# A range check of the softmax sums, with a branch to a short f32 path, at the end of a gated recurrence with soft mixture of experts

## The chip, the cores and the metric

The kernel runs on one core of one Trainium2 chip. The time is device microseconds of that core, the median of three runs. The profile is of one execution, and its times count from the start of its span.

## The reference, cut to what matters

Four sequences of 5056 tokens with 256 channels go through a gated linear recurrence. Its output feeds a soft mixture of 8 experts with 4 slots each, so 32 slots. Every slot takes a softmax over all 20224 tokens, every token one over the 32 slots.

```python
f = lower_bound + (1 - lower_bound) * sigmoid(f_logit);  i = 1 - f
for t in range(S):                       # S = 5056, B = 4, D = 256
    h = f[:, t] * h + i[:, t] * x[:, t];  y[:, t] = h
x = y.reshape(B * S, D)
logits = x @ phi                         # phi: 256 x 32, drawn at 0.05
d = exp(logits - logits.max(0));  d /= d.sum(0) + 1e-9
slot_in = (d.T @ x).reshape(8, 4, D)
slot_out[e] = maximum(slot_in[e] @ w1[e], 0) @ w2[e]      # 1024 hidden
c = exp(logits - logits.max(1));  c /= c.sum(1) + 1e-9
out = c @ slot_out                       # 20224 x 256, f32
```

The input x is drawn at 0.1 times a standard normal, f_logit around 2, lower_bound between 0.4 and 0.7.

## The kernel before, in words

The tokens go through in groups of 512 for each sequence. VectorE runs the recurrence as scans along time, with channels on partitions (L345), and TensorE turns tiles between tokens and channels (L263, L277, L358). The kernel takes its exponentials **without subtracting a maximum**: `etall` holds exp(logits) in bf16 for all tokens, with a sequence's 32 slots on 32 partitions. Two kinds of sums are kept of them. Each row sum, over the 32 slots of a token, is inverted and held in `rrow`, a tile of 128 x 40 x 4 f32. The column sums, over the tokens, are collected by group in `csum` and added up in `cs1` (L670). The order of all instructions is written out by hand (`manual_schedule`), and each engine works through its own queue.

From about 122 us the experts' weights arrive, and the slots' outputs are computed. The last weights are in at 140.48; then TensorE ends `so_ps` (L749), VectorE makes `slot_pre` and `slot_so` (L746, L747) and `slot_out` (L784), and GpSimd `slot_bd`. From there on the output is made. A piece of it is one small product of 32 or 64 slots with the exponentials (L813, L850), scaled by `rrow` on the way from PSUM to an output tile in turns by ScalarE and VectorE (L855, L858), and stored by SyncE's DMA queue. The helper `whole` makes the output of one sequence, `couple` that of two, for 2048 tokens; `couple` writes a tile `oc` of 128 x 2 x 16 x 256 f32 and issues two stores of 2048 KB, one for each sequence (L870). The last three calls of `couple` come last in the program, so its last two stores are those of the last call, first sequence then second. The tiles come from the pool `osb` with three buffers, the PSUM tiles from `pout` with eight.

Behind the last store the program leaves through line 927 (the exit of the tile context). There SyncE waits for all outstanding transfers and for the other engines, ten wait instructions in the built program, then drains, and two barriers over the five engines follow. Between the barriers GpSimd clears the semaphores.

```python
cs1 = ew.tile([P, 1], F32, name="cs1")                    # L669
nc.vector.tensor_reduce(cs1, csum, AX.X, ALU.add)
...
for i in range(end):                                      # end = 2
    for j in range(B // 2):
        if i or j < B // 2 - 1:
            couple(i, j)
```

Of the kernel before, what the change touches and what calls it, by code (L numbers as in the profile page):

```python
# [14 lines left out]
PSUM = bass.MemoryType.PSUM  # L15


@with_exitstack
def kernel(
# [58 lines left out]
    lbs = consts.tile([P, 4, DC], F32, name="lbs")  # L78
    omlb, nomlb = lbs[:, 0], lbs[:, 1]
# [43 lines left out]
    rrow = store.tile([P, n_grp * R, B], F32, name="rrow")  # L123
# [50 lines left out]
    with tc.tile_pool(name="sp2", bufs=3) as sp2, \  # L174
# [21 lines left out]
        xs, fs, sts, uts, pss, psus, hs, hps, hts, lgs, ets = ({} for _ in range(11))  # L196
# [438 lines left out]
        hid, wide = cleared["hid"], cleared["wide"]  # L635
        hid = hid.rearrange("p (f e s) -> p f e s", f=FC, s=NS)
# [17 lines left out]
        for o in range(DC):  # L654
            nc.tensor.matmul(sin_ps[:, o], slot_v[:, o], rep[:, 0],
                             start=True, stop=True, skip_group_check=True)

    with tc.tile_pool(name="ew", bufs=1) as ew, \
# [5 lines left out]
        sin = [ew.tile([P, NS], BF16, name=f"sin{o}") for o in range(DC)]  # L664
# [1 line left out]
        nc.scalar.activation(sin[1], sin_ps[:, 1], ACT.Copy, scale=omlb[:, ds(1, 1)])  # L666
        row_sums(8, 14)

        cs1 = ew.tile([P, 1], F32, name="cs1")  # L669
        nc.vector.tensor_reduce(cs1, csum, AX.X, ALU.add)  # L670


# [22 lines left out]
        for q in range(E // Q):  # L695
# [47 lines left out]
        for j in range(Q):  # L743
            for fc in range(FC):
                if j == Q - 1 and fc == half:
# [5 lines left out]
                                 start=(j, fc) in ((0, 0), (Q - 1, half)),  # L751
# [45 lines left out]


    held.close()
    with tc.tile_pool(name="osb", bufs=3, reuse_waits="tile") as osb:  # L800

        def by_vector(ob, op, scale):
            nc.vector.tensor_tensor(ob, op, scale.broadcast_to(list(ob.shape)), ALU.mult)

        def by_scalar(ob, op, scale):
            for i in range(ob.shape[1]):
                nc.scalar.activation(ob[:, i], op[:, i], ACT.Copy, scale=scale[:, i])  # L807

        def share(op, i, b, r, k):
            t0, n_r = blocks[i]  # L810
            ew = etall[ds(b * NS, NS), ds(t0, P * n_r)].rearrange("s (p r) -> s p r", r=n_r)
            for j in range(k):
                nc.tensor.matmul(op[:, j], ew[:, :, r + j], slot_out[ds(b * NS, NS)],  # L813
                                 start=True, stop=True, skip_group_check=True)

        def scale_of(i, b, r, k):
            return rrow[:, ds(blocks[i][0] // P + r, k), ds(b, 1)]

        def rows_of(i, b):
            t0, n_r = blocks[i]  # L820
            return out[ds(b * S + t0, P * n_r)].rearrange("(p r) d -> p r d", r=n_r)

        pout = ctx.enter_context(tc.tile_pool(name="pout", bufs=8, space=PSUM, reuse_waits="tile"))

        def whole(i, b, pieces, ends):
            n_r = blocks[i][1]
            dst = rows_of(i, b)
            ob = osb.tile([P, n_r, D], F32, name="ob", tag="ob")
            done = pieces[0][1]
            for j, r, k in pieces:  # L830
                op = pout.tile([P, 2, D], F32, name="op", tag="op")
                share(op, i, b, r, k)
                (by_vector, by_scalar)[j](ob[:, ds(r, k)], op[:, ds(0, k)],
                                          scale_of(i, b, r, k))
                if r + k in ends:
                    q = ds(done, r + k - done)
                    nc.sync.dma_start(out=dst[:, q], in_=ob[:, q])
                    done = r + k

        def couple(i, j, ends=()):  # L840
            t0, n_r = blocks[i]
            ends = ends or (n_r,)
            ew = etall[ds(j * 2 * NS, 2 * NS), ds(t0, P * n_r)].rearrange(
                "s (p r) -> s p r", r=n_r)
            scale = rrow[:, ds(t0 // P, n_r), ds(2 * j, 2)]
            ob = osb.tile([P, 2, n_r, D], F32, name="oc", tag="oc")
            done = 0
            for r in range(n_r):
                op = pout.tile([P, 2, D], F32, name="op", tag="op")
                nc.tensor.matmul(op.rearrange("p u d -> p (u d)"), ew[:, :, r],  # L850
                                 slot_bd[ds(j * 2 * NS, 2 * NS)].rearrange("s u d -> s (u d)"),
                                 start=True, stop=True, skip_group_check=True)
                if r % 7 in (1, 4, 6):
                    for u in range(2):
                        nc.scalar.activation(ob[:, u, r], op[:, u], ACT.Copy,  # L855
                                             scale=scale[:, r, ds(u, 1)])
                else:
                    nc.vector.tensor_tensor(  # L858
                        ob[:, :, r], op,
                        scale[:, r].unsqueeze(2).broadcast_to([P, 2, D]), ALU.mult)  # L860
                if r + 1 in ends:
                    q = ds(done, r + 1 - done)
                    if done:
                        both = out[ds(2 * j * S, 2 * S)].rearrange(
                            "(u t) d -> u t d", u=2)[:, ds(t0, P * n_r)].rearrange(
                            "u (p r) d -> p u r d", r=n_r)
                        nc.sync.dma_start(out=both[:, :, q], in_=ob[:, :, q])
                    else:
                        for u in range(2):
                            nc.sync.dma_start(out=rows_of(i, 2 * j + u)[:, q],  # L870
                                              in_=ob[:, u, q])
                    done = r + 1

        def rest():
            n_p = B // 2
            ob = osb.tile([P, n_p, D], F32, name="ob", tag="ob")
            dst = out.rearrange("(b t) d -> t b d", b=B)
            for j in range(n_p):
                k = ds(j * 2 * NS, 2 * NS)
                op = pout.tile([P, 2, D], F32, name="op", tag="op")  # L880
# [51 lines left out]
```

## Time and profile before

| | |
|---|---|
| median of 3 runs | 196.48 us (196.40 to 197.11) |
| the profiled execution's own time | 196.48 us |
| its span | 194.7 us (194.69), 1.79 less |
| busy: TensorE, VectorE, ScalarE, GpSimd | 149.7, 145.7, 140.9, 104.9 us |
| read from and written to HBM | 58.23 and 20.71 MB, 405 GB/s over the span |
| last compute instruction starts | 174.56 us |
| last store issued | 175.11 us |

The page of the profile cuts the span in 40 slices of 4.87 us and gives the busy share of each engine in tenths. "SPq" is SyncE's instruction queue, "DVE" is VectorE, "ACT" ScalarE, "PE" TensorE's matmuls and "PEld" its weight loads, "POOL" GpSimd. A row of waits names who waited, for whom, the sum in us, how often, and the longest. In the answer for one line, the three numbers behind a count are the shortest, median and longest duration in ns, followed by the start of the first and of the last.

### The profile page before, as it was taken

To read this page: it belongs to the slowest core of one execution; us is meant where nothing else is said; L and a number is where in the kernel's file an instruction comes from. 1 tells how busy PE (TensorE), PEld (TensorE's weight loads), DVE (VectorE), ACT (ScalarE), POOL (GpSimd) and SP (SyncE) were. 2 spreads that over 40 slices of the span, in tenths; PEclk is the share of its full clock that TensorE was granted. 3 is DMA by queue.
4 is the path that set the end of the run, shared out by engine and by line. 5 is a ranking of instruction groups with operands and counts; after the bars stand their busy time and mean duration, and the time that the engine had idled before them with its cause. 6 is when DMAs were issued, how large, how long until landed. Compare 5 with 4: busy or idle time off the path is not lost.

```text
span 194.7 us, 3288 instructions
## 1 busy us (share of the span) xinstructions
PE 149.7 (77%) x1203; PEld 103.9 (53%) x1204; DVE 145.7 (75%) x197; ACT 140.9 (72%) x204; POOL 104.9 (54%) x82
## 2 busy tenths in 40 slices
PE   2777797988999889789789868999898999970000
PEld 1655666765786767657576746567775333210000
DVE  2259899999799999999999999525199799760000
ACT  3199678899998999999988797644269987770000
POOL 2369679774999778884978988484030000000000
PEclk9999999999999999999999999999999555555555
DMA  5999999999999999999999999999949999999995
GB/s 204 415 418 423 427 429 421 428 431 380 351 429 422 411 328 422 431 425 353 382 415 407 264 223 214 213 215 213 181 175 422 429 432 431 431 431 431 431 431 219
DMA packets 13281, 70.75 MB, mean 363 GB/s; under 512 B 1473, under 2 KB 2242, under 8 KB 9298
## 3 DMA queue, kind: packets, MB, share of 16 engines
q1 hardware_dynamic: 10352, 62.13, 76.7%
q0 software_dynamic: 2912, 8.42, 21.9%
q8 instruction: 9, 0.15, 0.3%
q14 instruction: 6, 0.05, 0.1%
q10 hardware_dynamic: 2, 0.00, 0.0%
HBM read 58.23 MB, written 20.71 MB: 405 GB/s over the span
## 4 chain that ended last, share of the span: by engine, by line
DVE 24%; DMA 22%; PE 18%; ACT 11%; issue 8%; POOL 7%; ACTq 0%; POOLq 0%; DVEq 0%
DVE h L345 16%; DMA w_t<-in_moe_w_dram 9%; PE op L850 9%; POOL u_t L253 6%; DMA x_t<-in_x_dram 5%; DMA w_sb<-in_moe_w_dram 5%; ACT oc L855 5%; DVE ht L377 4%; DVE h L337 3%; DMA base<-in_lower_bound_dram 2%; PE sp L263 2%; PE hp L358 2%; ACT ob L807 2%; PE up L277 2%; ACT s_t L242 2%
## 5 line engine op out<-in xcount | busy, mean ns | idle before, releaser
L253 POOL TENSOR_TENSOR u_t<-s_t,x_t 128x1024 bf16<-128x1024 bf16 (+1 forms) x39 | 82.4, 2130 | 20.8 <-ACT s_t L242 15.3
L345 DVE TENSOR_TENSOR_SCAN h<-a,h,up 128x512 bf16<-128x512 f32 x64 | 77.7, 1265 | 2.5 <-PE up L277 2.2
L242 ACT ACTIVATE s_t<-f_t 128x2048 bf16<-128x2048 f32 (+2 forms) x23 | 38.4, 1673 | 4.0 <-DMA f_t<-in_f_logit_dram 3.8
L358 PE MATMUL hp<-base,h 128*128 128x128 f32 (+1 forms) x160 | 29.0, 304 | 10.8 <-DVE ht L377 7.6
L358 PEld LDWEIGHTS hp<-base,h 128*128 128x128 f32 (+1 forms) x160 | 22.3, 207 | 19.7 <-DVE ht L377 12.4
L850 PE MATMUL op<-slot_bd,etall 64*128 64x512 bf16 x62 | 25.2, 561 | 1.5 <-ACT ob L807 0.3
L304 ACT ACTIVATE a<-sp,lbs 128x1024 f32<-128x1024 bf16 x24 | 25.4, 1114 | 0.7 <-PE sp L263 0.6
L855 ACT ACTIVATE oc<-op,rrow 128x256 f32<-128x256 f32 x54 | 22.1, 512 | 4.0 <-PE op L850 3.9
L858 DVE TENSOR_TENSOR oc<-op,rrow 128x512 f32<-128x512 f32 x35 | 22.0, 685 | 2.4 <-PE op L850 2.3
L263 PE MATMUL sp<-base,s_t 128*128 128x128 f32 x158 | 21.7, 278 | 1.1 <-ACT a L320 0.6
L277 PE MATMUL up<-base,u_t 64*128 64x64 f32 x220 | 20.4, 230 | 1.1 <-POOL u_t L253 1.0
L194 PE MATMUL slot_ps<-base 128*128 128x256 f32 x62 | 20.5, 438 | 0.0
L263 PEld LDWEIGHTS sp<-base,s_t 128*128 128x128 f32 x158 | 18.3, 144 | 3.0 <-ACT a L320 1.3
L277 PEld LDWEIGHTS up<-base,u_t 64*128 64x128 f32 x220 | 16.1, 138 | 6.5 <-issue 2.8
L320 ACT ACTIVATE a<-sp,lbs 128x512 f32<-128x512 bf16 (+1 forms) x18 | 14.1, 836 | 7.4 <-PE sp L263 7.4
L850 PEld LDWEIGHTS <-etall 64*128 64x128 bf16 x62 | 9.0, 150 | 16.7 <-issue 12.0
L377 ACT COPY ht<-hp 128x512 f32<-128x512 f32 (+1 forms) x20 | 11.7, 583 | 4.8 <-PE hp L358 4.8
L377 DVE COPY ht<-hp 128x512 f32<-128x512 f32 (+1 forms) x20 | 13.4, 668 | 1.3 <-PE hp L358 1.3
L345 DVE TENSOR_TENSOR_SCAN h<-a,up 128x512 bf16<-128x512 f32 x8 | 9.4, 1210 | 3.7 <-PE up L263 3.6
L194 PEld LDWEIGHTS slot_ps<-base 128*128 128x128 f32 x62 | 10.9, 207 | 2.2 <-issue 1.1
L391 PE MATMUL lg<-h,phi 128*32 128x512 bf16 (+1 forms) x80 | 9.6, 389 | 0.0
L263 PE MATMUL up<-base,u_t 128*128 128x128 f32 x48 | 7.9, 290 | 2.1 <-POOL u_t L253 1.1
(120 smaller groups left out, 151.8 us busy)
## 6 DMA issues: line engine op xcount, KB each, us to landing
f_t<-in_f_logit_dram SPq DMA_DIRECT2D x12, 1024.0 KB, 11.6
x_t<-in_x_dram SPq DMA_DIRECT2D x12, 1024.0 KB, 10.1
out_dram<-oc SPq DMA_DIRECT2D x6, 2048.0 KB, 14.3
w_sb<-in_moe_w_dram POOLq DMA_DIRECT2D x14, 512.0 KB, 10.3
f_t<-in_f_logit_dram SPq DMA_DIRECT2D x12, 512.0 KB, 8.9
x_t<-in_x_dram SPq DMA_DIRECT2D x12, 512.0 KB, 8.7
out_dram<-ob SPq DMA_DIRECT2D x1, 2048.0 KB, 10.4
f_t<-in_f_logit_dram SPq DMA_DIRECT2D x2, 896.0 KB, 13.2
```

The costliest lines, as they stand in the source:

```text
L194: nc.tensor.matmul(slot_bank[:, 1], ident_f, wide_ident, start=False, stop=False, skip_group_check=True)
L242: nc.scalar.activation(s_t, f_t, ACT.Sigmoid, scale=-1.0)
L253: nc.gpsimd.tensor_tensor(uts[n][:, :r], s_t[:, :r], x_t[:, :r], ALU.mult)
L263: nc.tensor.transpose(ps[:, :, r], t[:, r], ident_f)
L277: nc.tensor.transpose(v[..., r], t(r)[k].bitcast(F32), ident_f[k, k])
L304: nc.scalar.activation(a, sp[:, :, :, :, o], ACT.Identity, scale=nomlb[:, ds(o, 1)], bias=1.0)
L345: nc.vector.tensor_tensor_scan(h[:, :T, o], decays[n // 2, o][:, n % 2, :T], up[:, :T, o], hs[number(g - 1, b)][:, ds(used(g - 1) - 1, 1), ...
L358: nc.tensor.transpose(hp[:n_p, r], hw[:, :n_p, r], ident_f)
L377: copy(hts[g][:n_p, b].rearrange("p r d -> p (r d)").bitcast(F32), hps.pop(n)[:n_p].rearrange("p r c -> p (r c)"))
L850: nc.tensor.matmul(op.rearrange("p u d -> p (u d)"), ew[:, :, r], slot_bd[ds(j * 2 * NS, 2 * NS)].rearrange("s u d -> s (u d)"), start=Tru ...
L855: nc.scalar.activation(ob[:, u, r], op[:, u], ACT.Copy, scale=scale[:, r, ds(u, 1)])
L858: nc.vector.tensor_tensor(ob[:, :, r], op, scale[:, r].unsqueeze(2).broadcast_to([P, 2, D]), ALU.mult)
```

## The change

Behind the last `couple`, the 159 sums and inverse sums that the kernel used (all columns of `rrow` up to the column sum, which is now written there) are clamped to 1e-12 to 1e12 and compared with themselves. A one-column memset into the output tile of the last call comes next; it has to wait until the store that reads this part of the tile, the last but one, has landed. Then the comparison is reduced over the columns, a matmul with ones adds up the 128 partitions, and the sum is turned into one flag. All five engines load the flag into a register and branch. If it is set, `guarded` computes everything again in f32 with running maxima, in three loops (79, 8 and 79 passes). If it is not, each engine goes through a short block that waits for its own semaphore's count and raises it by what the second path would have added; SyncE does so for the eight semaphores of the stores, one wait each. Then it jumps behind the code of the second path, to the exit, which now has twelve waits for SyncE. The PSUM pool `pout` is opened beside `osb` and closes with it.

```diff
+SAFE = 1e12
+
+@with_exitstack
+def guarded(ctx, tc, x, f_logit, moe_phi, moe_w1, moe_w2, out, lbs):
...
+    with tc.For_i(0, n_t, 1) as i:
...
+        nc.vector.tensor_tensor(new, new, top, ALU.max)
+        nc.vector.tensor_scalar_mul(minus, new, -1.0)
+        nc.scalar.activation(shrink, top, ACT.Exp, bias=minus)
+        nc.scalar.activation(e, lg_ps, ACT.Exp, bias=minus, accum_out=part)
...
+    with tc.For_i(0, E, 1) as i:
...
+    with tc.For_i(0, n_t, 1) as i:
...
-        cs1 = ew.tile([P, 1], F32, name="cs1")
+        cs1 = rrow[:, n_grp * R - 1, ds(B // 2, 1)]
         nc.vector.tensor_reduce(cs1, csum, AX.X, ALU.add)
...
-    with tc.tile_pool(name="osb", bufs=3, reuse_waits="tile") as osb:
+    with tc.tile_pool(name="osb", bufs=3, reuse_waits="tile") as osb, \
+         tc.tile_pool(name="pout", bufs=8, space=PSUM, reuse_waits="tile") as pout:
...
-        pout = ctx.enter_context(tc.tile_pool(name="pout", bufs=8, space=PSUM, reuse_waits="tile"))
...
                     done = r + 1
+            return ob
...
         for i in range(end):
             for j in range(B // 2):
                 if i or j < B // 2 - 1:
-                    couple(i, j)
+                    ob = couple(i, j)
+
+        n_v = (n_grp * R - 1) * B + B // 2 + 1
+        sums_of = rrow.rearrange("p q b -> p (q b)")[:, ds(0, n_v)]
+        clamped, one, fine = base[:, ds(0, n_v)], base[:, ds(D, 1)], base[:, ds(D + 1, 1)]
+        unsafe = base[ds(0, 1), ds(D + 2, 1)].bitcast(mybir.dt.int32)
+        nc.vector.memset(one, 1.0)
+        nc.vector.tensor_scalar(clamped, sums_of, 1.0 / SAFE, SAFE, ALU.max, ALU.min)
+        nc.vector.tensor_tensor(clamped, clamped, sums_of, ALU.is_equal)
+        nc.vector.memset(ob[:, 0, 0, ds(0, 1)], 0.0)
+        nc.vector.tensor_reduce(fine, clamped, AX.X, ALU.min)
+        fine_ps = pout.tile([P, 2, D], F32, name="fine_ps", tag="op")[ds(0, 1), 0, ds(0, 1)]
+        nc.tensor.matmul(fine_ps, fine, one, start=True, stop=True)
+        nc.vector.tensor_scalar(unsafe, fine_ps, float(P), None, ALU.is_lt)
+
+    beyond = nc.values_load(unsafe, min_val=0, max_val=1)
+    with tc.If(beyond != 0, preferred_fallthrough_block=False):
+        guarded(tc, x, f_logit, moe_phi, moe_w1, moe_w2, out, lbs)
```

More of the change, by code (lines that the diff above doesn't have):

```diff
@@ L15, with guarded, half @@
 PSUM = bass.MemoryType.PSUM
+SAFE = 1e12
+@with_exitstack
+def guarded(
+    ctx: ExitStack,
+    tc: tile.TileContext,
+    x: bass.AP,
+    f_logit: bass.AP,
+    moe_phi: bass.AP,
+    moe_w1: bass.AP,
+    moe_w2: bass.AP,
+    out: bass.AP,
+    lbs,
+):
+    nc = tc.nc
+    B, S, D = x.shape
+    E, _, F = moe_w1.shape
+    NS = moe_phi.shape[1]
+    SPE = NS // E
+    P = 128
+    DC = D // P
+    FC = F // P
+    T = P // 2
+    J = B // 2
+    W = B * T
+    n_t = S // T
+    assert n_t * T == S
+    omlb, nomlb = lbs[:, 0], lbs[:, 1]
+    one = ctx.enter_context(tc.tile_pool(name="g_one", bufs=1))
+    ps = ctx.enter_context(tc.tile_pool(name="g_ps", bufs=1, space=PSUM))
+    ident = one.tile([P, P], F32, name="g_ident")
+    make_identity(nc, ident)
+    phi = one.tile([P, DC, NS], F32, name="g_phi")
+    nc.sync.dma_start(out=phi, in_=moe_phi.rearrange("(p o) s -> p o s", o=DC))
+    for o in range(DC):
+        nc.vector.tensor_scalar_mul(phi[:, o], phi[:, o], omlb[:, ds(o, 1)])
+    mask = one.tile([NS, E], F32, name="g_mask")
+    nc.vector.tensor_reduce(mask, ident[:NS, :NS].rearrange("s (e k) -> s e k", k=SPE), AX.X, ALU.add)
+    lgs = one.tile([NS, B * S], F32, name="g_lgs")
+    acc = one.tile([NS, D], F32, name="g_acc")
+    so = one.tile([NS, D], F32, name="g_so")
+    carry = one.tile([P, DC, B], F32, name="g_carry")
+    col = one.tile([NS, 8], F32, name="g_col")
+    top, new, minus, shrink, den, part, on = (col[:, ds(i, 1)] for i in range(7))
+    nc.vector.memset(top, -3e38)
+    nc.vector.memset(den, 0.0)
+    nc.vector.memset(acc, 0.0)
+    nc.vector.memset(so, 0.0)
+    nc.vector.memset(carry, 0.0)
+    f_t = one.tile([P, J, D], F32, name="g_f")
+    x_t = one.tile([P, J, D], F32, name="g_x")
+    a = one.tile([P, DC, B, T], F32, name="g_a")
+    h = one.tile([P, DC, B, T], F32, name="g_h")
+    h_t = one.tile([P, J, D], F32, name="g_h_t")
+    e = one.tile([NS, W], F32, name="g_e")
+    e_t = one.tile([P, J, NS], F32, name="g_e_t")
+    s_ps = ps.tile([P, DC, B, T], F32, name="g_s_ps")
+    u_ps = ps.tile([P, DC, B, T], F32, name="g_u_ps")
+    h_ps = ps.tile([P, J, D], F32, name="g_h_ps")
+    sl_ps = ps.tile([NS, D], F32, name="g_sl_ps")
+    lg_ps = ps.tile([NS, W], F32, name="g_lg_ps")
+    e_ps = ps.tile([P, FC * NS], F32, name="g_e_ps")
+    def half(j):
+        return ds(j * P, P)
+    with tc.For_i(0, n_t, 1) as i:
+        for src, dst in ((f_logit, f_t), (x, x_t)):
+            for j in range(J):
+                nc.sync.dma_start(out=dst[:, j], in_=src[ds(2 * j, 2), ds(i * T, T)])
+        nc.scalar.activation(f_t, f_t, ACT.Sigmoid, scale=-1.0)
+        nc.vector.tensor_tensor(x_t, x_t, f_t, ALU.mult)
+        for src, dst in ((f_t, s_ps), (x_t, u_ps)):
+            v = src.rearrange("t j (c o) -> t j o c", o=DC)
+            for j in range(J):
+                for o in range(DC):
+                    nc.tensor.transpose(
+                        dst[:, o, ds(2 * j, 2)].rearrange("c b t -> c (b t)"), v[:, j, o], ident)
+        for o in range(DC):
+            nc.scalar.activation(a[:, o], s_ps[:, o], ACT.Identity,
+                                 scale=nomlb[:, ds(o, 1)], bias=1.0)
+        for b in range(B):
+            for o in range(DC):
+                nc.vector.tensor_tensor_scan(h[:, o, b], a[:, o, b], u_ps[:, o, b],
+                                             carry[:, o, ds(b, 1)], ALU.mult, ALU.add)
+        nc.vector.tensor_copy(carry, h[:, :, :, T - 1])
+        for o in range(DC):
+            nc.tensor.matmul(lg_ps, phi[:, o], h[:, o].rearrange("c b t -> c (b t)"),
+                             start=o == 0, stop=o == DC - 1)
+        nc.scalar.copy(lgs[:, ds(i * W, W)], lg_ps)
+        nc.vector.tensor_reduce(new, lg_ps, AX.X, ALU.max)
+        nc.vector.tensor_tensor(new, new, top, ALU.max)
+        nc.vector.tensor_scalar_mul(minus, new, -1.0)
+        nc.scalar.activation(shrink, top, ACT.Exp, bias=minus)
+        nc.scalar.activation(e, lg_ps, ACT.Exp, bias=minus, accum_out=part)
+        nc.vector.tensor_copy(top, new)
+        nc.vector.scalar_tensor_tensor(den, den, shrink, part, ALU.mult, ALU.add)
+        for j in range(J):
+            nc.tensor.transpose(e_ps[:, ds(j * NS, NS)], e[:, half(j)], ident[:NS, :NS])
+            for o in range(DC):
+                nc.tensor.transpose(h_ps[:, j, half(o)],
+                                    h[:, o, ds(2 * j, 2)].rearrange("c b t -> c (b t)"), ident)
+        nc.scalar.copy(e_t.rearrange("t j s -> t (j s)"), e_ps[:, ds(0, J * NS)])
+        nc.vector.tensor_copy(h_t, h_ps)
+        for j in range(J):
+            nc.tensor.matmul(sl_ps, e_t[:, j], h_t[:, j], start=j == 0, stop=j == J - 1)
+        nc.vector.scalar_tensor_tensor(acc, acc, shrink, sl_ps, ALU.mult, ALU.add)
+    nc.vector.tensor_scalar_add(den, den, 1e-9)
+    nc.vector.reciprocal(den, den)
+    nc.vector.tensor_scalar_mul(acc, acc, den)
+    sin = one.tile([P, DC, NS], F32, name="g_sin")
+    for o in range(DC):
+        nc.tensor.transpose(e_ps[:, ds(o * NS, NS)], acc[:, half(o)], ident[:NS, :NS])
+        nc.vector.tensor_scalar_mul(sin[:, o], e_ps[:, ds(o * NS, NS)], omlb[:, ds(o, 1)])
+    w1_t = one.tile([P, DC, F], F32, name="g_w1")
+    w2_t = one.tile([P, FC, D], F32, name="g_w2")
+    hid = one.tile([NS, F], F32, name="g_hid")
+    hid_t = one.tile([P, FC, NS], F32, name="g_hid_t")
+    H = F // 2
+    hid_ps = [t.rearrange("c o b t -> c (o b t)")[:NS] for t in (s_ps, u_ps)]
+    with tc.For_i(0, E, 1) as i:
+        nc.sync.dma_start(out=w1_t, in_=moe_w1[ds(i, 1)].rearrange("e (p o) f -> p (e o) f", o=DC))
+        nc.sync.dma_start(out=w2_t, in_=moe_w2[ds(i, 1)].rearrange("e (p f) d -> p (e f) d", p=P))
+        nc.vector.tensor_copy(on, mask[:, ds(i, 1)])
+        for k in range(2):
+            for o in range(DC):
+                nc.tensor.matmul(hid_ps[k], sin[:, o], w1_t[:, o, ds(k * H, H)],
+                                 start=o == 0, stop=o == DC - 1)
+            nc.vector.tensor_scalar(hid[:, ds(k * H, H)], hid_ps[k], 0.0, on, ALU.max, ALU.mult)
+        for fc in range(FC):
+            nc.tensor.transpose(e_ps[:, ds(fc * NS, NS)],
+                                hid.rearrange("s (p f) -> s f p", f=FC)[:, fc], ident[:NS, :NS])
+        nc.vector.tensor_copy(hid_t.rearrange("p f s -> p (f s)"), e_ps)
+        for fc in range(FC):
+            nc.tensor.matmul(sl_ps, hid_t[:, fc], w2_t[:, fc], start=fc == 0, stop=fc == FC - 1)
+        nc.vector.tensor_tensor(so, so, sl_ps, ALU.add)
+    lg = one.tile([NS, W], F32, name="g_lg")
+    c = one.tile([NS, W], F32, name="g_c")
+    cols = one.tile([P, 2, J], F32, name="g_cols")
+    with tc.For_i(0, n_t, 1) as i:
+        nc.vector.tensor_copy(lg, lgs[:, ds(i * W, W)])
+        for j in range(J):
+            nc.tensor.transpose(e_ps[:, ds(j * NS, NS)], lg[:, half(j)], ident[:NS, :NS])
+        v = e_ps[:, ds(0, J * NS)].rearrange("t (j s) -> t j s", s=NS)
+        nc.vector.tensor_reduce(cols[:, 0], v, AX.X, ALU.max)
+        nc.vector.tensor_tensor(e_t, v, cols[:, 0].unsqueeze(2).broadcast_to([P, J, NS]),
+                                ALU.subtract)
+        nc.scalar.activation(e_t, e_t, ACT.Exp)
+        nc.vector.tensor_reduce(cols[:, 1], e_t, AX.X, ALU.add)
+        nc.vector.tensor_scalar_add(cols[:, 1], cols[:, 1], 1e-9)
+        nc.vector.reciprocal(cols[:, 1], cols[:, 1])
+        nc.vector.tensor_tensor(e_t, e_t, cols[:, 1].unsqueeze(2).broadcast_to([P, J, NS]),
+                                ALU.mult)
+        for j in range(J):
+            nc.tensor.transpose(lg_ps[:, half(j)], e_t[:, j], ident)
+        nc.scalar.copy(c, lg_ps)
+        for j in range(J):
+            nc.tensor.matmul(h_ps[:, j], c[:, half(j)], so, start=True, stop=True)
+        nc.vector.tensor_copy(h_t, h_ps)
+        for j in range(J):
+            nc.sync.dma_start(out=out.rearrange("(b t) d -> b t d", b=B)[ds(2 * j, 2), ds(i * T, T)],
+                              in_=h_t[:, j])
```

## The prediction

> **What bounds the kernel now.** The change sits at the end of the program, so I read the profile from its end. First the slices of the span, for what runs there:
>
> ```profile
> PE   2777797988999889789789868999898999970000
> DVE  2259899999799999999999999525199799760000
> ACT  3199678899998999999988797644269987770000
> ...
> DMA  5999999999999999999999999999949999999995
> GB/s 204 415 418 423 427 429 421 428 431 380 351 429 422 411 328 422 431 425 353 382 415 407 264 223 214 213 215 213 181 175 422 429 432 431 431 431 431 431 431 219
> ```
>
> In the last four slices (4.87 us each) no compute engine works, and from slice 31 on the DMA engines move 422 to 432 GB/s without a gap. The end is set by how fast the output leaves. Then the waits of SyncE's queue, and the instructions of line 927 (the exit of the program) on SyncE in 176.3 to 176.75, in 176.9 to 193.7 and in 193.7 to 194.7 us:
>
> ```profile
> SPq L927 <- DMA out_dram<-oc: 16.9, 4, 4.9
> ```
>
> ```profile
> L927 SPq EVENT_SEMAPHORE  x6: 17/28/28, 176.4 to 176.7; - x6
> ...
> L927 SPq EVENT_SEMAPHORE  x3: 28/28/28, 179.2 to 189.0; - x3
> ...
> L927 SPq EVENT_SEMAPHORE  x3: 17/17/28, 193.8 to 194.6; - x3
> L927 SPq DRAIN  x3: 7/7/13, 193.8 to 194.2; - x3
> ```
>
> SyncE issues its last store at 175.11 and then stands in ten exit waits. Six pass at once; their records start at 176.379 to 176.689, which is 0.062 us for each. Four wait for the last four stores: they are released at 179.25, 184.05, 188.97 and 193.78. So the last store lands 4.81 us after the last but one. Behind 193.78 only a drain (193.85) and two rounds of the barrier over all engines follow, 0.91 us to the end at 194.69. The profiled execution took 196.48 us, 1.79 more than its span; 196.48 is also the median of the three runs, so a change of the span is added to it directly.
>
> **The change, part by part.** The second path is not run here: logits are sums of 256 products of a state near 0.1 or less and 0.05, so each exponential is near 1, a sum over 32 slots is near 32, and one over 5056 tokens near 5056; all lie within 1e-12 to 1e12. What is paid is the check and the way around the path.
>
> *Up to 175 us* the built program has the same instructions in the same order on every engine, with the same waits. The column sum is written into a free column of `rrow` instead of a tile of its own (the L670 reduction, 0.155 us, both times). Four register moves more stand on SyncE ahead of the opening barrier; by the 0.062 us above that is 0.25 us, and SyncE arrives there 0.56 us before GpSimd, the last. Nothing.
>
> *First half of the check* (a memset, a clamp and a compare of 128x159 f32 on VectorE) comes behind VectorE's last work at 174.44. The nearest rows are the memsets (0.059 us) and L792's 128x256 f32 (0.425 us): under 1 us in all, under cover of 18 us of stores. Without them it would cost that 1 us.
>
> *The wait and the second half.* VectorE then stands in a memset that waits for the last store but one, so until 188.97. Behind it on VectorE is only the check; TensorE's matmul of the check and each engine's register load wait for that. All stores were issued by then, so no DMA is queued behind it. The chain from 188.97 goes by the nearest rows, from the answers for single lines (ns, shortest/median/longest):
>
> ```profile
> L95 DVE MEMSET pair_ones<- x1: 59/59/59, 0.9 to 0.9; 128x1 uint32 x1
> L104 DVE TENSOR_REDUCE lbs<-base x1: 151/151/151, 2.6 to 2.6; 128x1 f32<-128x4 f32 x1
> L111 PEld LDWEIGHTS lb_ps<-base x2: 191/201/211, 6.2 to 6.3; 1*128 1x128 f32 x2
> L111 PE MATMUL lb_ps<-base x2: 253/264/275, 6.2 to 6.4; 1*128 1x1 f32 x2
> L112 DVE TENSOR_SCALAR lbs<-lb_ps x1: 159/159/159, 6.7 to 6.7; 128x2 f32<-128x2 f32 x1
> L501 ACT ACT_TABLE_LOAD  x1: 1283/1283/1283, 0.7 to 0.7; - x1
> ```
>
> and one of the chain of waits (start, us, what):
>
> ```profile
> 1.96 4.24 DMA base<-in_lower_bound_dram
> ```
>
> Memset 0.06; reduction of 159 columns between L104's 0.15 and L792's 0.43, I take 0.30; load and matmul 0.20+0.26, rounded to 0.50; result to a flag 0.16; four handovers at 0.05, 0.20; range test, assertion and branch, four sequencer instructions at 0.062, 0.25. That is 1.47 us without the register load, which no row shows. Its bounds are a semaphore instruction (0.02) and the 1 KB that ScalarE's queue reads from memory (4.24). I take 1.3, from the table load that an engine makes for itself: that is also a read which one engine waits for, and no queue stands in between. So the check ends at 188.97 + 1.47 + 1.3 = 191.74, and 2.04 us remain to 193.78. It is hidden under the last store; at the bound of 4.24 it would end at 194.68, 0.90 late.
>
> *What is moved behind the last store.* This is the cost. On the path not taken, SyncE waits once for each of eight store semaphores (the last is released at 193.78 as before), then jumps over the second path to the exit, and only there stands in its exit waits, now twelve, all fulfilled. Before, nine of the ten were passed ahead of 193.78. Twelve at 0.062 is 0.74 us. The jump: no taken jump is in the trace. It costs at least a sequencer step, 0.05, and I take as its upper bound for code that is already on the chip one 8 KB code packet, 0.31; I take 0.15, nearer to the step, since nothing is then moved. [...]
>
> *Code fetched by the other engines' jumps.* The trace has code packets of 8 KB (six, 0.31 us each) and of 16 KB (nine, 0.88 to 1.04 us), at the times at which an engine passes 128 (TensorE 256) instructions more: VectorE had started 66 and 195 at two of them, ScalarE 63 and 190. Four engines jump forward near 191.7 into the next such piece, and can so call for one more each while the last store is under way. Of that store's 16 shares 15 are in by 192.97, one at 193.76. On one of the 15, a packet has 0.79 us of cover: 0.31 costs nothing, 0.96 costs 0.17; on the late one each costs its whole length. From 0 to 0.96; I take 0.1.
>
> Sum: 0.74 + 0.15 + 0.1 = 0.99, rounded 1.0. Span 194.69 to 195.7, time 196.48 to **197.5 us**.
>
> **The rivals.**
>
> *The jump leaves the loaded code.* Then SyncE waits for a code fetch behind the last store. [...] Against it: at TensorE's fetches work does not pause (52 starts in the 3 us after the one at 60.01), so the packet is the piece after the next, and two pieces are at hand. SyncE had started 59 or 81 instructions at its fetch (65.0 or 95.8 us), which covers it to about 314 or 336; it jumps from about 143 over some 140 to about 280. For it: that count leaves 34 to 56. Price: a transfer with the queues empty, between the shortest store (256 KB, 2.0 us) and the 4.24 above: 196.48 + 0.9 + 2.0 = 199.4, up to 201.6. Chance 0.13.
>
> *The check outlasts the last store.* It decides from a register load above 3.3 us (1.3 + 2.04). At 4.24 it is 0.90 late, and seven of the eight waits (0.43) come behind it too: 197.5 + 1.3 = 198.8. Chance 0.09: the row of 4.24 reads the memory, the check's word lies in a tile.
>
> *A code packet meets the late share of the last store.* 197.5 - 0.1 + 0.96 = 198.4. Chance 0.08: one of 16.
>
> *Not slower: the tiles behind the freed column run faster.* The old tile took 32 bytes; eight tiles behind it (`hi`, `em`, `gain`, `slot_so`, `slot_pre` and others) move down by 32, to starts that divide by 64. Between the last weights (140.48) and the first store (143.17) lie L746, L747 and L784 with 0.49 us each, and any lead there reaches the end, since the stores then run without a gap. Were all three as short as L792 (0.425), it is 3 x 0.06 = 0.2, time 197.3; to be no slower it must be 1.0 of 2.7 us. Nothing in the rows shows a penalty to lose. Chance 0.06, with a gentler exit than I count: 196.4.
>
> *It does not do what it says*: a column of `rrow` that holds no sum would send it down the second path, over 160 loop passes, hundreds of us. All 159 columns read are written (39 x 4, two of the remainder, the column sum). 0.01.
>
> **How the numbers follow.** About 0.5% (0.98 us) is what a measurement of this kernel can tell from no change. My likeliest case (0.63, own range 196.9 to 198.0) lies on that bound, so half of it, 0.31, counts as slower, and 0.32 as same. Slower: 0.31 + 0.13 + 0.09 + 0.08 + 0.01 = 0.62. Of the not-slower rival 0.05 is faster, 0.01 same: same 0.33. The range runs from 196.7 (leaving out that rival) to 199.4, the low end of the fetch; left out are 0.06, half of the fetch and the second path, 0.14, and some tails.
>
> **What would show it.** Right: stores landing as before to 0.2 us; register loads over before the last landing; twelve exit waits of 0.06 us behind it, and near 1.8 us from it to the end instead of 0.91. A gap of 2 us or more between SyncE's last wait for a store and its first exit wait shows the fetch; register loads ending after the last landing show the late check; a last store over 5 us after the one before shows the packet. A stage before 175 us that differs would make the whole argument wrong.

## The result and the profile after

| | before | after |
|---|---|---|
| median of the timed runs | 196.48 us (196.39 to 197.11) | 197.98 us (197.78 to 199.07) |
| ratio, with its 95% interval | 1 | 1.0078 (1.0056 to 1.0100) |
| profiled execution: own time, span | 196.48, 194.69 us | 198.2, 196.43 us |
| last store lands, drain, end | 193.76, 193.85, 194.69 us | 194.17, 195.54, 196.43 us |

The changed kernel is 1.5 us slower, and timed once more (`a3_after_timed`, below) it came to 1.0085 (1.0067 to 1.0103). The prediction was 197.5 us, in a range of 196.7 to 199.4. First the slices of the span after, answering to those shown of before:

```profile
PE   2866889998999889889789867999999999970000
DMA  5999999999999999999999999999869999999992
GB/s 204 416 419 422 428 429 422 427 427 360 376 427 425 398 343 422 427 423 371 361 422 410 234 214 214 214 213 214 130 259 418 427 442 427 427 427 427 427 437 110
```

The store stage (from slice 31 on) is as dense as it was; of its slices only the last differs clearly, with 110 GB/s instead of 219, since the tail behind the last store takes more of it. Then the waits of SyncE's queue from 176 us on, after (who waited, for whom, us, times, longest):

```profile
SPq L1088 <- DVE base L1086: 12.4, 1, 12.4
SPq L1089 <- SPq L1089: 2.0, 1, 2.0
```

Before, SyncE stood in four exit waits for the last four stores. Now it waits 12.4 us for the flag, in which three of the stores land, and then 2.0 us in line 1089, the short way around the second path, for the last one. These 2.0 us are the cover of the check: it could have been so much longer. The instructions of line 1089 on SyncE, and of line 1116 (the exit) on SyncE between 194.7 and 195.52 us:

```profile
L1089 SPq EVENT_SEMAPHORE  x8: 17/17/17, 191.8 to 194.2; - x8
L1089 SPq COMPARE_BRANCH  x2: 38/46/53, 191.7 to 194.3; - x2
```

```profile
L1116 SPq EVENT_SEMAPHORE  x12: 28/28/28, 194.8 to 195.5; - x12
```

The branch not taken comes at 191.69, seven of the eight waits at 191.80 to 192.23, the eighth is released at 194.188 by the last store. Behind it: the jump at 194.258, the first exit wait at 194.774, twelve of them, the drain at 195.540, the end at 196.43. Before, the drain came 0.07 us behind the same landing. So behind the last landing the kernel got 0.52 us for the jump and 0.77 us for twelve waits that were fulfilled long before.

The check itself lies in front of that, hidden:

```profile
L1083 DVE TENSOR_REDUCE base<-base x1: 313/313/313, 189.2 to 189.2; 128x1 f32<-128x159 f32 x1
L1085 PEld LDWEIGHTS fine_ps<-base x2: 79/80/82, 189.7 to 189.7; 128*1 128x1 f32 x2
L1085 PE MATMUL fine_ps<-base x2: 163/164/164, 189.7 to 189.7; 128*1 128x1 f32 x2
L1086 DVE TENSOR_SCALAR base<-fine_ps x1: 145/145/145, 189.9 to 189.9; 1x1 int32<-1x1 f32 x1
```

```profile
L1088 SPq TENSOR_LOAD <-base x1: 1147/1147/1147, 190.2 to 190.2; - x1
```

From the landing of the last store but one (189.21) to SyncE's branch (191.69) it takes 2.48 us.

**Reading the two profiles at equal clock.** The last store lands 0.41 us later in the profile after than in the one before, and 0.24 of it is there at the first store already, long ahead of the check. In some executions of either program TensorE is granted half its clock for 3.4 us from about 81.5 us on (81.54 to 84.95 in the profile after). The windows from 80 to 86 us (busy time of PE, PEld, DVE, ACT, POOL with counts, granted clock, DMA share, GB/s), of before, of after, of the unaltered kernel before run once more (`b2_before_again`) and of the unaltered changed one (`a2_after_again`):

```profile
80.00:86.00 6.00, 5.16 (x44) 3.64 (x43) 6.00 (x6) 5.53 (x6) 5.10 (x3) 1.00 1.00 423
```

```profile
80.00:86.00 6.00, 5.41 (x34) 3.97 (x31) 4.48 (x5) 4.82 (x5) 4.05 (x3) 0.72 1.01 427
```

```profile
80.00:86.00 6.00, 5.16 (x34) 3.81 (x32) 4.66 (x5) 4.52 (x5) 3.83 (x3) 0.72 1.01 426
```

```profile
80.00:86.00 6.00, 5.16 (x45) 3.63 (x43) 6.00 (x6) 5.52 (x6) 5.03 (x3) 1.00 1.01 427
```

The clock is 1.00 in the first and the last, 0.72 in the two between, and the first store lands at 145.18 and 145.08 against 145.42 and 145.56. Each kernel has both kinds. Compared at equal clock, the spans differ by 196.06 - 194.69 = 1.37 us (both without the dip) and 196.43 - 195.07 = 1.36 us (both with it). That is the size of the change in the profiles: 0.77 waits + 0.52 jump + 0.05 (from the drain to the end, 0.89 instead of 0.84) + 0.03 later landing; in sum 1.37.

The small 0.03 is itself a difference of two things. In both pairs the changed kernel's first store lands earlier, by 0.10 and 0.14 us, and from there to the last landing it takes 48.72 to 48.75 us instead of 48.59, since the last store is stretched. From the first landing to the end it is 49.51 us in both profiles of the kernel before and 50.97 to 51.01 in the three of the changed one: 1.46 to 1.50 us more. Whether the lead at the first store belongs to the change is not shown.

The timed executions say the same. The record has the mean granted clock of each of them, and in the 14 profiles here it is 0.863 to 0.866 in the six with the dip and 0.875 to 0.889 in the eight without. Taking 0.868 or less as the sign of a dip, 16 of the 67 executions of the kernel before that have a clock on record show it, with a median of 196.92 us against 196.46 for the rest; of the changed kernel it is 5 of 14, with 198.23 against 197.91. So at like clock the change costs 1.45 us without the dip and 1.31 with it. The mean is a sign only: it also depends on when the clock falls to a half at the end, at 146 to 152 us in the profiles (151.51 before, 146.40 after).

### The profile page after: what moved, and what is told of

The parts are those of the page before. It is cut to its first block, busy times and chain, and to the rows that moved or that the text cites. A ratio compares the mean times of both kernels' runs of the same rounds, so it can differ in the third digit from the quotient of the medians.

```text
span 196.4 us, 3339 instructions
## 1 busy us (share of the span) xinstructions
PE 153.0 (78%) x1205; PEld 105.8 (54%) x1206; DVE 147.1 (75%) x203; ACT 141.5 (72%) x204; POOL 104.8 (53%) x82
## 4 chain that ended last, share of the span: by engine, by line
PE 31%; DVE 21%; issue 13%; ACT 13%; POOL 9%; DMA 8%; POOLq 0%; ACTq 0%; DVEq 0%
DVE h L517 12%; PE op L1021 10%; POOL u_t L425 7%; DMA x_t<-in_x_dram 6%; PE hp L530 3%; PE sp L435 3%; DVE ht L549 3%; DVE h L509 3%; ACT oc L1026 3%; PE up L449 2%; ACT a L476 2%; DMA base<-in_lower_bound_dram 2%; PE op L986 2%; ACT s_t L414 2%; PE so_ps L921 2%
## 5 line engine op out<-in xcount | busy, mean ns | idle before, releaser
L530 PE MATMUL hp<-base,h 128*128 128x128 f32 (+1 forms) x160 | 29.5, 308 | 10.6 <-DVE ht L549 7.2
L1021 PE MATMUL op<-slot_bd,etall 64*128 64x512 bf16 x62 | 26.1, 590 | 0.8 <-DVE ob L976 0.2
L435 PE MATMUL sp<-base,s_t 128*128 128x128 f32 x158 | 22.6, 286 | 1.5 <-ACT a L492 1.0
L435 PEld LDWEIGHTS sp<-base,s_t 128*128 128x128 f32 x158 | 19.1, 148 | 3.1 <-ACT a L492 1.4
```

The lines of the kernel that those rows point to most:

```text
L435: nc.tensor.transpose(ps[:, :, r], t[:, r], ident_f)
L530: nc.tensor.transpose(hp[:n_p, r], hw[:, :n_p, r], ident_f)
```

## The experiments

The theory: the whole price is what stands behind the last landing, that is jump and waits; check and wait for the last store but one are hidden, and code packets cost little. Against it stand three others: the check costs something by itself, the distance of the jump brings a fetch, or the code packets that the jumps call for hold up the last store.

**The check without the branch.**

```diff
-    beyond = nc.values_load(unsafe, min_val=0, max_val=1)
-    with tc.If(beyond != 0, preferred_fallthrough_block=False):
-        guarded(tc, x, f_logit, moe_phi, moe_w1, moe_w2, out, lbs)
```

> All of the check, up to the flag, but no register load, no branch and no second path. Theory (the loss is what SyncE runs behind the last landing: a jump of 0.5 us and twelve exit waits of 0.77 us in place of one): nothing is behind the landing, 196.5 us, within 0.2 of before. Rival 1 (the moved tiles or the check itself shift the stores; in the profile they begin 0.24 us later): 196.7 to 196.8. Rival 2 (waiting for the last store but one and what hangs on it disturbs the last store): 196.6, with the last store 4.9 to 5.0 us behind the one before instead of 4.8.

Measured: 196.62 us, 1.0002 (0.9989 to 1.0015), span 194.66. SyncE stands in its exit waits for the stores again, ahead of the last landing:

```profile
SPq L1113 <- DMA out_dram<-oc: 10.1, 3, 4.8
```

One of its exit waits now ends with the check's flag, at 189.81, long before the last landing (193.74). The check up to its flag costs nothing; all of the 1.5 us belongs to the register load, the branch and what they move.

**The check without its wait for a store.**

```diff
-        nc.vector.memset(ob[:, 0, 0, ds(0, 1)], 0.0)
```

> The change without the memset that waits for the last store but one: the check runs at 176 us, the branch near 178. SyncE still waits for all stores on the way around and jumps behind the last. Theory: the cost stays, 197.7 to 197.9 (less the 0.15 by which the last store was late, since code packets now come earlier). Rival (the wait for the store and the check behind it are the cost): 196.5 to 196.8.

Measured: 199.1 us, 1.0124 (1.0107 to 1.0142): slower than the change as it is, by about 1 us, where no loss was expected. Now SyncE is through with its branch at 179.7 us and stands in line 1088, the short way around, for three stores:

```profile
SPq L1088 <- SPq L1088: 15.2, 3, 5.7
```

One of these waits takes 5.7 us; the longest before took 4.9. The DMA queues between 179 and 186 us (packets, MB, share of 16 engines) show with what:

```profile
q8 instruction: 1, 0.02, 0.9%
q14 instruction: 3, 0.02, 0.9%
```

Four engines jump at 179.0 to 179.3, and four code packets start at 183.36 to 184.02 us, where one store's shares end and the next one's begin. The first of these two stores lands 5.97 us behind the one before it instead of 4.80, the two after it follow at 4.65 and 4.82 (4.93 and 4.96 in the changed kernel). From 179 us to the last landing that is 0.75 us more than in the changed kernel's profile with the same dip; another 0.37 are there before any of the packets and stay unexplained. In the changed kernel the same four packets come at 192.73 to 192.92, when the shares of the last store end, and that store lands 4.96 us behind its predecessor. So the wait for the last store but one is no cost but a protection: it puts the jumps, and the packets that follow them, to a place where no store comes behind.

**The check waits for the last store.**

```diff
-        nc.vector.memset(ob[:, 0, 0, ds(0, 1)], 0.0)
+        nc.vector.memset(ob[:, 1, 0, ds(0, 1)], 0.0)
```

> The memset waits for the last store instead of the last but one, so nothing covers the second half of the check. Theory (the check is hidden in the change, and takes 2.55 us from landing to SyncE's first wait): behind the landing come 2.55 + eight waits 0.57 + jump 0.52 + twelve waits 0.77 + 0.9, in place of 0.07 + 0.84: 4.4 us over before, 200.7 to 201.1. Rival (the check is not what the store covers, something else holds the branch): 198.0 as with the change.

Measured: 200.5 us, 1.0198 (1.0181 to 1.0216), a little under the range expected. The chain is now all behind the landing (193.88): branch at 195.69 (1.81), eight waits to 196.29 (0.60), jump to 196.88 (0.59 with the step ahead of it), twelve waits to 197.65 (0.77), end at 198.71 (1.06); in sum 4.83 us. So the cover of the last store is worth about 2.5 us to the change. One row is much shorter than in the changed kernel:

```profile
L1088 SPq TENSOR_LOAD <-base x1: 472/472/472, 194.8 to 194.8; - x1
```

It is 0.47 us with the stores at rest, against 1.15 while they run. That is most of the reason why the check took 1.81 us here and not the 2.55 expected.

**A short second path on SyncE.** Its body is eight small stores, which keep eight waits in the way around; the code to jump over is short.

```diff
     with tc.If(beyond != 0, preferred_fallthrough_block=False):
-        guarded(tc, x, f_logit, moe_phi, moe_w1, moe_w2, out, lbs)
+        for k in range(8):
+            nc.sync.dma_start(out=out[ds(k * P, P), ds(0, 2)], in_=lbs[:, 0])
```

> Check and branch as in the change, but the second path holds only eight tiny stores by SyncE's queue (so it would not repair anything): SyncE's eight waits on the way around and twelve exit waits stay, the jump becomes short and calls for no code. Theory with a jump that costs 0.5 us by itself: 197.7 to 197.8 (1.3 for jump and waits). Theory with a jump whose 0.5 us come from its distance: 197.3 to 197.4 (0.77 for the waits and 0.1). Rival 2 (code packets on the last store): the last store returns to 4.8 us behind the one before, at either time.

Measured: 197.93 us (197.45 to 198.26), 1.0067 (1.0049 to 1.0086). By that ratio alone the length of the path would matter little. The profile is plainer. SyncE's instructions of line 1089 are the same as in the changed kernel:

```profile
L1089 SPq EVENT_SEMAPHORE  x8: 17/17/17, 191.8 to 194.1; - x8
L1089 SPq COMPARE_BRANCH  x2: 38/46/53, 191.7 to 194.2; - x2
```

The exit's waits (line 1117, 194 to 195.2 us) begin earlier:

```profile
L1117 SPq EVENT_SEMAPHORE  x12: 17/28/28, 194.4 to 195.1; - x12
```

From the jump (194.21) to the first exit wait (194.39) pass 0.19 us, not 0.52, and no code packet is left of the five that came with the change (the page has 9 and 6 of the two kinds, as before, against 10 and 10). The span is 196.04, with the dip of the clock; against `b2_before_again` with the same dip it is 0.97 us more: 0.19 for the jump, 0.75 for the waits, 0.03 for the rest. The times at like clock agree: three of the six executions show the sign of the dip, and the medians are 0.16 us (with it) and 0.32 us (without) below the changed kernel's. So the price of a jump depends on what it jumps over, 0.33 us here. Whether the distance decides or that the target lies in another piece of code, these runs do not separate: in all of them both go together.

The last store lands 4.90 us behind its predecessor here too, against 4.81 before: most of the 0.12 to 0.15 us by which the changed kernel stretches it is there without any code packet. It is not there where no register load falls into the last store (4.82 without the branch, 4.79 with the wait for the last store). What of the register loads and the branch stretches it was not tried.

**The second path's transfers on GpSimd's queue.** Then SyncE's block on the way around holds no wait for the stores, and they can stand in the exit, as before.

```diff
-    nc.sync.dma_start(out=phi, in_=moe_phi.rearrange("(p o) s -> p o s", o=DC))
+    nc.gpsimd.dma_start(out=phi, in_=moe_phi.rearrange("(p o) s -> p o s", o=DC))
...
```

(and so all five transfers of `guarded`.)

> The whole change, but the second path loads and stores by GpSimd's queue instead of SyncE's. Then SyncE has no store semaphore to raise on the way around, jumps before the last store has landed, and passes eleven of its twelve exit waits ahead of it. Theory: 196.5 to 196.8 (only code packets and noise are left of the 1.5). Rival 1 (shift of the stores): 196.7 to 197.0. If the jump or the check cost anything in itself and not by its place: 197.3 or more.

Measured: 197.37 us, 1.0043 (1.0027 to 1.0059): better than the change, not as good as expected. None of its six executions shows the sign of the dip, so it is to be compared with 197.91 us, the changed kernel's median without it: 0.54 us less. Both costs are indeed gone from the tail: SyncE is in the exit at 192.48 and has passed its fulfilled waits by 193.15; only one wait ends behind the landing.

```profile
SPq L1116 <- DMA out_dram<-oc: 1.8, 1, 1.8
```

But the landing is late, 194.96, 5.75 us behind the store before. The store's data are out at 193.66, and at that moment two code packets begin. The DMA queues from 192.6 to 195.9:

```profile
q14 instruction: 4, 0.03, 3.3%
q8 instruction: 1, 0.02, 2.4%
```

All five that came with the change are now ahead of the landing, SyncE's own among them; the store's signal comes 1.30 us behind its last data instead of 0.47 before and 0.54 in the changed kernel. Of the 1.29 us saved behind the landing, about 0.8 are given back ahead of it.

**The second path laid first in the code.** Here the long jump is at the test and none behind the landing.

```diff
-    with tc.If(beyond != 0, preferred_fallthrough_block=False):
+    with tc.If(beyond != 0, preferred_fallthrough_block=True):
```

> The change with one flag turned: the second path's code stands first, so the engines make their long jump at the test itself, ahead of the last landing, and the way around lies next to the exit. Theory (the jump behind the landing cost 0.52 us only because it was long; twelve waits 0.77 stay): 197.5 to 197.7 against 198.0. If SyncE's code packet, now called for ahead of the landing, holds back the last store's signal as in the run with the path on GpSimd's queue: 198.2 to 198.4. Rival (the 0.52 us belong to any jump behind the landing): 197.9 to 198.1.

Measured: 198.12 us, 1.0080 (1.0062 to 1.0099), no better than the change. The jump did move: SyncE branches at 191.45 and goes on at 191.97 (0.52 again), and from SyncE's release by the last store (194.80) to the first exit wait there is 0.07 us. By its time alone the run would fit the rival as well; the profile decides. One packet of code starts between 193.3 and 194.9 us:

```profile
q14 instruction: 1, 0.01, 1.8%
```

It begins at 193.38, where the data of the last store end, and the store's signal comes at 194.78, 1.40 us behind. In the changed kernel the packets of the other four engines come ahead of the landing and do not delay it as much, and SyncE's comes at 195.31, behind it. So the packet that hurts should be SyncE's own, on the DMA engine of the one share in 16 that ends the last stores about 0.8 us after the other fifteen (193.76 against 192.97 before). The trace names the DMA engine neither of a packet nor of a share; the run with 96 drains below tests this.

**A short path on GpSimd's queue**: both remedies together.

```diff
-        guarded(tc, x, f_logit, moe_phi, moe_w1, moe_w2, out, lbs)
+        for k in range(8):
+            nc.gpsimd.dma_start(out=out[ds(k * P, P), ds(0, 2)], in_=lbs[:, 0])
```

> As the run with the second path on GpSimd's queue, but the path is only eight tiny stores there (so it would not repair anything): the jumps stay inside the code piece at hand, and no engine calls for code. Theory (what was left of 0.9 us in that run is the two code packets that start as the last store's data ends and hold back its landing signal, 1.30 us behind the last packet instead of 0.5): 196.5 to 196.7, no code packet behind 143 us. Rival (five register loads, the assertion and the branch cost 0.9 us in themselves): 197.2 to 197.5.

Measured: 196.91 us, 1.0022 (1.0010 to 1.0034). No added code packet (the page):

```profile
q8 instruction: 9, 0.15, 0.3%
q14 instruction: 6, 0.05, 0.1%
```

and 0.06 us from SyncE's release (194.43) to its drain. So with neither waits nor a long jump behind the landing nor a packet ahead of it, 1.1 of the change's 1.5 us are gone (the same without the dip: 196.82 us, 1.09 below the changed kernel). Against `b2_before_again`, at equal clock, 0.45 us of span are left: 0.26 for the landing, of which 0.15 is there from the first store on, and 0.2 between drain and end, where GpSimd's own drain of 1.78 us in the exit (from 192.89) now ends late.

**SyncE's code fetched early**, by padding ahead of an early store, on top of the GpSimd version, in two sizes.

```diff
+        for _ in range(80):          # 96 in the second
+            nc.sync.drain()
         nc.sync.dma_start(
```

> The second path on GpSimd's queue, and 80 empty drains on SyncE while it waits for the first store at about 100 to 143 us: they move SyncE's jump and its target into one piece of code, so that SyncE calls for no packet. Theory with SyncE's packet as the one that holds the landing signal back: 196.8 to 197.0, four code packets instead of five behind 143 us, and the signal 0.5 us behind the last store's last packet. Theory with GpSimd's packet: 197.3 to 197.4 as without the drains, and 1.3 us. Rival (the drains themselves cost): 197.5 or more, with a first store behind 145.7.

> As with 80 drains, but 96. With 80, SyncE reached the end of its piece of code (its 208th instruction, by the records) one step behind the register load, so the packet came all the same; with 96 it gets there near 155 us, and the jump, its target and the exit all lie in the next piece. Theory (SyncE's packet sits on the DMA engine that ends last, and holds back the last store's signal by 0.8 to 0.9 us): its packet stands near 155 to 165 us, the signal comes 0.5 us behind the last store's last packet, and the time falls to 196.8 to 197.1 (0.3 for the packet inside the stores). Rival (GpSimd's packet, which starts at the same moment, does it): 1.3 us behind, 197.4 to 197.7.

With 80 it is 197.66 us, 1.0051 (1.0032 to 1.0069). This one missed its aim: SyncE passed the edge of its piece of code (its 208th instruction, by the records) only beside the register load, the packet came at 193.85, and the signal again 1.30 us behind the last data. With 96 it is 197.83 us, 1.0064 (1.0048 to 1.0080). Here SyncE's packet came at 158.39 us, as the DMA queues from 150 to 163 us show:

```profile
q14 instruction: 1, 0.01, 0.2%
```

The signal of the last store came 0.49 us behind its data, as without a packet, although another engine's packet starts there too (194.21). So SyncE's packet is what held it up. It also points to the DMA engine that the packet uses, that of the late share: at the store ahead of the packet this share trails the others by 0.31 us, behind it by 1.1 to 1.2 (159 to 165 us); with 80 drains, where no packet falls there, it stays at 0.32.

Yet the run was expected at 196.8 to 197.1 and is 0.46 us slower than without padding, for two reasons. First, the packet set the late share back for good: at the last store it trails by 1.48 us where it was 0.79 before, so the last store lands at 194.74, hardly earlier than the 194.96 without padding. Second, the exit (line 1118, from 192 us):

```profile
L1118 POOLq DRAIN  x3: 46/107/1837, 193.6 to 196.0; - x3
L1118 SPq DRAIN  x3: 7/7/7, 194.8 to 195.7; - x3
```

GpSimd's drain of 1.84 us begins at 193.59, since the check itself started 0.53 us later, and ends at 195.43, 0.55 after SyncE's (194.88); the barrier waits for it.

**Both kernels unaltered, and the changed one timed again.**

> The changed kernel unaltered, one look. In its first profile the granted clock is at half from 81.5 to 85.0 us, and the first store lands 0.24 us later than before. If that dip is the cause and comes and goes from run to run: without a dip the first store lands at 145.2 and the span is 196.1 to 196.2; with it as in the first profile. Rival (the changed code shifts the stores itself): 145.4 without a dip too.

> The kernel before unaltered, one look, for the same question. Dip as the cause: with a dip the first store lands near 145.4 and the span is 194.9 to 195.0, without one 145.2 and 194.7. Rival: 145.2 whatever the clock does.

> The changed kernel unaltered, timed in the same way as the experiments, for a comparison with the version whose path is on GpSimd's queue (1.0043, 1.0027 to 1.0059). Theory (1.36 us between the spans of two profiles with equal clocks): a ratio of 1.007, 1.005 to 1.009, above 1.0043. Rival (the version on GpSimd's queue is no gain): 1.0045 or less.

Measured: 197.82 us (span 196.06, no dip) for the changed kernel and 196.84 (span 195.07, with the dip) for the one before; timed like the experiments, the changed kernel has 198.17 us, 1.0085 (1.0067 to 1.0103). The first two serve the pairs at equal clock above. They also show how little one execution of each tells: these two differ by 0.98 us, the same kernels at equal clock by 1.37.

No version is faster than the kernel before. Of those that hold the second path, the one with its transfers on GpSimd's queue is the best (1.0043 against 1.0078 and 1.0085 for the change as it is).

## Why the prediction was right, point by point

- **Exit waits behind the last landing**: 0.74 predicted, 0.77 measured (194.774 to 195.540). The mechanism and the count were right, and it is the larger half of the cost.
- **The jump**: the term that was mis-sized. 0.15 was taken, with 0.31 as the upper bound "for code that is already on the chip"; it took 0.52. That is nearly all of what the forecast of 1.0 us lacks to the 1.4 of the profiles. The time of 197.98 us, and 198.17 when timed again, lies at the upper edge of the 196.9 to 198.0 given for the likeliest case; the whole range is wider for another reason, the fetch, which did not come. The row was chosen wrongly: from a sequencer's step (0.047 us on SyncE before, from its wait at 175.059 to its store at 175.106) and a code packet's transfer (0.31) no bound on a branch follows. Over a short path SyncE's jump took 0.19, near the value taken; over `guarded` the five engines took 0.37 (TensorE) to 0.56 (VectorE).
- **Code packets**: 0.1 predicted within 0 to 0.96. Four came ahead of the landing, as foreseen, SyncE's behind it. The store was stretched by 0.12 and 0.15 in the two pairs at equal clock (4.93 and 4.96 against 4.81), but 0.09 of that the short path has without a packet, so 0.03 to 0.06 is left for the packets. The value of 0.1 looks right by luck: another cost, which the prediction did not have, fills most of it. And the small value holds for this order of events only: the upper end is real, as 0.8 to 0.9 us in three experiments in which SyncE's packet met the late share (the signal 1.30, 1.40 and 1.30 us behind the last data, not 0.47).
- **The check is hidden**: 2.77 us predicted from landing to branch, 2.48 measured; 2.04 us of cover predicted, 2.0 measured. The reduction (0.31 for 0.30), the flag (0.15 for 0.16) and the register load (1.15 for 1.3) came out near. For the last, that is luck: the row it was taken from is another kind of load, and the same register load took 0.47 with the stores at rest. Load and matmul were half of what was taken (0.25 for 0.50): the row taken was that of another shape (1*128, 0.20 and 0.26 us; here 128*1, 0.08 and 0.16). The version without the branch shows that the check costs nothing.
- **The sum**: 0.99 + 0.37 (jump) + 0.03 (waits) + 0.05 (exit) - 0.07 (later landing: 0.03 for 0.1) = 1.37, as the profiles have at equal clock. The medians differ by 1.5 to 1.7, those at like clock by 1.31 and 1.45. So part of the gap is that more of the changed kernel's executions show the sign of the dip (5 of 14 against 16 of 67); what is left to 1.37 (0.08 without the dip, -0.06 with it) is less than single executions at like clock differ by (197.78 to 198.17 for the changed kernel without it).
- **The rivals.** *The jump leaves the loaded code*: no gap of 2 us. Where the memset with its wait was taken out, four engines jump at 179 us and go on 0.37 to 0.56 us later, though the packets come only 4 us after that; so what they jump to was there. That a target outside the loaded code would make SyncE wait was the author's assumption; no run has such a target, so it is neither shown nor refuted. *The check outlasts the last store*: 2.0 us to spare. *A packet meets the late share*: not in the changed kernel, since SyncE's jump is itself behind the landing; where the jump or SyncE's waits were moved ahead of it, it did, at 0.83 to 0.93 us, near the 0.96 foreseen. The chance of one in 16 was reasoned wrongly, though: in the runs here it is no draw among 16 engines but SyncE's packet each time, so the order of events decides. *The shifted tiles run faster*: the first store lands at 145.08 with the dip absent against 145.18, and 145.42 against 145.56 with it, so at most 0.1 to 0.14 us. *The second path* was not run.
- The line on what would show it asked for stores landing "as before to 0.2 us"; they were 0.21 to 0.27 off in the first pair of profiles, and the last one 0.41. The 0.21 to 0.27 go with the clock, not the change, as the equal pairs show; the other 0.15 is the stretch of the last store, which comes with the change. "Near 1.8 us" from the landing to the end was 2.24, by the jump.

## What to carry to other kernels

What stood behind the last landing counted in full here, even twelve waits whose condition was met long ago (0.77 us): this branch near the end was priced by what its way around does on the queue that ends last (1.29 us with the jump), not by the test, which had 2.0 us to spare. Moving that ahead of the landing was only a gain as far as the code that it called for did not meet the store in return (with the path on GpSimd's queue about 0.8 of the 1.29 us were given back), so look where code packets lie beside the last data. And compare profiles of one program with one another before two programs: here a dip of the clock, which comes and goes in either program, made 0.37 of the 1.74 us between the first two spans.

## What the runs showed of the hardware that was not expected

- A taken jump over `guarded` took 0.37 (TensorE), 0.44 (ScalarE), 0.46 (GpSimd), 0.52 (SyncE) and 0.56 us (VectorE) to the next instruction in the changed kernel; over the short path SyncE's took 0.19. The branch not taken took 0.09 to 0.11 there, on TensorE 0.15.
- Loading one word from a tile into a register took 1.11 to 1.22 us in the changed kernel, while the last store runs, and 0.46 to 0.55 us where the check waits for the last store and the stores rest.
- Where SyncE's code packet came as the last store's data ended, that store's signal came 1.30 us (path on GpSimd's queue, and with 80 drains) and 1.40 us (path first) behind the last data instead of 0.47. In the middle of the stores, with 96 drains, the late share of a store went from 0.31 to 1.17 us behind the others, and the later landings wait for it (1.48 us at the last store).
- One of a store's 16 shares lands behind the other fifteen in the store stage, before by 0.33 us at 158.6 and 0.82 us at 179.2. That it is one DMA engine each time, the one that SyncE's code comes through, is read from the run with 96 drains; no trace names it.
- GpSimd's first drain in the exit took 1.84 us in the changed kernel (192.04 to 193.89, ahead of the last landing) and 1.78 us over the short path on its queue, where it ends late; with 96 drains (1.84 us, to 195.43) the barrier waits for it.
- TensorE's granted clock falls to a half at about 81.5 to 85 us in some executions of one and the same program; the first store then lands 0.34 to 0.38 us later. Four of the experiments have it as late (145.31 to 145.61) with no dip; the cause of that is open.
